# A pre-norm transformer block on one core: the last two MLP sub-units as one group of four tiles, and the attention's GpSimd additions placed one VectorE instruction later

## The chip, the core and the metric

The kernel runs on one core of one Trainium2 chip. A core has five engines that each execute their own queue in order: TensorE (PE in the profile, its weight loads are PEld), VectorE (DVE), ScalarE (ACT), GpSimd (POOL) and SyncE (SP, which here only issues DMAs). They meet through semaphores. The metric is the device time of one execution in microseconds (us).

## The reference

One token stream of 2048 rows and 512 columns goes through a sliding dilated attention and then through an MLP with a squared ReLU, each behind a layer norm and each with a residual.

```python
B, S, D, H, F = 1, 2048, 512, 32, 1792      # head size 16, window 8, dilation 2
qkv = layernorm(x) @ wqkv                    # 2048 x 1536
idx = pos[:, None] - 2 * arange(8)           # eight keys for each row
logits = einsum("bhsd,bhswd->bhsw", q, k[idx]) * 16 ** -0.5   # masked where idx < 0
o = einsum("bhsw,bhswd->bhsd", softmax(logits), v[idx])
h = x + o @ wo
y = relu(layernorm(h) @ w1 + b1) ** 2        # 2048 x 1792
out = h + y @ w2 + b2
```

Everything is float32.

## The kernel before

**Tiles.** The 2048 rows are 16 tiles of 128 rows. Two tiles form a sub-unit `s`, 0 to 7 (`NS` = 8, `RI` = 2 tiles `j` in each). The hidden size of 1792 is 14 blocks `f` (`FB` = 14), the model size 512 is 4 blocks of 128 (`KB`).

**Products in three parts.** Each float32 operand is split into a high part (a cast on ScalarE, `hi`) and a low part (the difference, `lo`), and each product is three: high times high, high times low, low times high. So `mm3` (lines 172 to 177) issues 12 matmuls for 4 blocks. The names in the profile carry this: `hh`, `hl` are the parts of the transposed, normalized h, `rh`, `rl` those of the hidden activations, `oh`, `ol` those of the attention's output, `w_h`, `w_l` those of a weight.

**Phases.** First comes QKV: its products are stored to DRAM (`qkv_d`), and the attention loads windows of them back. The rest is a loop over sub-units (lines 675 to 711). In each, a slot `f` issues on TensorE `mlp1(s, f)` (12 matmuls, the weights stationary, 256 columns moving: both tiles side by side, into a `mm` bank) and, `LAG` = 3 slots behind, `mlp2(s, f - 3)` (6 matmuls of 512 columns into two accumulators `acc0`, `acc1`). Between `mlp1` and `mlp2` of a block stand on ScalarE ReLU, square and the cast `rh` (lines 512, 513, 115), and the difference `rl` on GpSimd (line 118; on VectorE for the last sub-unit, `HV`).

**What a sub-unit does for the next.** In slots 0 and 1 the loads of h, in slots 3 and 4 `o_T`, the transposes of the attention's output of `s + 1` (four PE transposes into a `tr` bank, of which there are two, shared with `wo`), in slots 6 and 7 `wo_product` (12 matmuls of 512 columns), a slot later `h_add` on VectorE with the norm's statistics, the norm's factor `rs` on GpSimd, and three slots after the product `hn` on ScalarE (`h_norm`). In the three slots after the last block `h_T` transposes `hn`, and ScalarE and VectorE make `hh` and `hl`, which the first product of the next sub-unit reads. `finish` (line 544) adds an accumulator to h and stores it; the accumulators exist once, so the next sub-unit's `mlp2` waits for it. `add_b2` adds the bias to h on GpSimd.

**The attention's stream.** `attention()` (lines 219 to 339) is a generator of VectorE work that runs beside the products: for each of 32 items two products with the keys (line 272), two sums (306, 320), softmax pieces, and two products with the values (`weigh`, line 283). What `weigh` makes is added up over the window by three GpSimd instructions, called **additions** here (line 292: two into `pr`, the last into `o`). There are three `pr` buffers. `pump` (line 343) draws from this stream at the end of a slot for as long as the VectorE time that it has counted is below the PE time counted; each piece of the stream counts `SLOW` = 1.1 times its nominal time. `o_T(s)` first draws the stream until sub-unit `s` is complete.

**Order.** The program is written by hand: `at(n, ...)` and `after(n, ...)` put a step into the slot `n` later, ahead of or behind the piece of attention that `pump` draws there. Each engine executes in the order in which its instructions were written.

**Buffers.** Fifteen `row` buffers (`ROWS`) hold h, hn, the parts of o and h, and one piece of w2. The attention has its own: `k`, `v` (2 each), `pr`, `o` (3 each), and the PSUM banks `qp`, `ex`.

Of the kernel before, what the change touches and what calls it, by code (L numbers as in the profile page):

```python
# [15 lines left out]
P = 128  # L16
# [13 lines left out]
LAG = 3  # L30
SLOW = 1.1
DELAY = 3
HV = 7
WJ = 2
# [4 lines left out]
def block_kernel(ctx, tc, x, wqkv, wo, w1, b1, w2, b2, out):  # L39
# [48 lines left out]
    late = {}  # L88
    now = {"slot": 0, "pe": 0.0, "dve": 0.0}

# [128 lines left out]
    def attention():  # L219
# [26 lines left out]
        for n in range(N + 1):  # L246
# [32 lines left out]
            def weigh(j):  # L279
                load_v(n - 1, j)  # L280
                vwin = window(vs[n - 1, j], s1, [DH, GH], [1, DH])
                p2 = att.tile([P, RI, W, GH, DH], F32, name="pr", bufs=3)
                nc.vector.tensor_tensor(  # L283
                    out=p2, in1=vwin, op=ALU.mult,
                    in0=e1[:, :, :, j * GH:(j + 1) * GH].unsqueeze(4).to_broadcast(
                        [P, RI, W, GH, DH]))
                c0 = (2 * gp1 + j) * GC
                w = W // 2
                while w:
                    dst = p2[:, :, :w] if w > 1 else o_t[s1][:, :, c0:c0 + GC].rearrange(  # L290
                        "p i (w h d) -> p i w h d", w=1, h=GH)
                    nc.gpsimd.tensor_tensor(out=dst, in0=p2[:, :, :w], in1=p2[:, :, w:2 * w],  # L292
                                            op=ALU.add)
                    w //= 2
                load_v(n, j)
                done[s1] += 1

# [34 lines left out]
            if new:  # L332
# [21 lines left out]

# [143 lines left out]
    def h_T(s, j):  # L498
        if j == 0:
            hT[s] = ([row("hh", (P, KB // 2, RI, P), F32R) for _ in range(2)],  # L500
                     [row("hl", (P, KB // 2, RI, P), F32R) for _ in range(2)])
        hh, hl = hT[s]
        tr = transposes(hn.pop((s, j)))
        hs_, ls_ = [t[:, :, j] for t in hh], [t[:, :, j] for t in hl]
        due.setdefault(now["slot"], []).insert(0, (hi_T, (tr, hs_)))
        at(0, lo_T, tr, hs_, ls_)

    hid = {}

    def hidden(s, f, ps):  # L510
        r = work.tile([P, RI * P], F32, name="r", bufs=2)
        nc.scalar.activation(r, ps, AF.Relu, bias=b1_sb[:, f:f + 1])  # L512
# [161 lines left out]

    for s in range(NS):
        acc = [psum.tile([P, D], F32, name=f"acc{j}") for j in range(RI)]
        for f in range(FB):
            more = 0.0
            if s + 1 < NS:
                if f in (0, 1):  # L680
                    at(0, load_h, s + 1, f)
                if f in (3, 4):
                    o_T(s + 1, f - 3)
                if f in (6, 7):
                    wo_product(s + 1, f - 6)
                    more = 2.6
            mlp1(s, f)
# [8 lines left out]
        if s + 1 < NS:
            for n, f in enumerate(range(FB - LAG, FB)):
                if n < RI:
                    h_T(s + 1, n)
                    after(0, add_b2, s + 1, n)  # L700
                mlp2(s, f, acc)
                end_slot(1.3)
        else:
            for j in range(RI):
                for f in range(FB - LAG, FB):
                    mlp2(s, f, acc, [j])
                    if j == 0:
                        end_slot(0.65)
        for j in range(RI):
# [25 lines left out]
```

## Time and profile before

| | us |
|---|---|
| median of 3 runs | 533.65 (533.29 to 534.02) |
| the profiled execution | 532.95 |
| its span, first to last instruction | 531.0 |
| sub-unit 1 begins on PE (chain of waits) | 207.67 |
| sub-units 2, 3, 4, 5, 6 | 254.34, 301.02, 347.69, 394.37, 441.04 |
| sub-unit 7 | 487.71 |
| last instruction, an addition on VectorE, ends | 527.93 |

The table's times of sub-units are read from the chain of waits, the list of what released what, followed back from the last instruction. Its pieces are counted there from one engine's release to the next; the timeline of PE counts an instruction from its issue, about 0.16 us earlier. A matmul's duration in the timeline contains its pipeline, so the distance between two starts is what it costs in a row of many. After the last instruction the span contains the store of the last tile.

### The profile page before, as it was taken

The page shows a single profiled execution, that of the slowest core. Times are in us where ns is not written, and L with a number is a line of the kernel's source. Part 1 is how long each engine was busy: PE and PEld are TensorE (multiplying, and loading weights), DVE is VectorE, ACT ScalarE, POOL GpSimd, SP SyncE. Part 2 cuts the span into 40 slices and gives each one's busy share as a digit, 9 for nine tenths or more (in the row PEclk, how much of TensorE's full clock was granted, in tenths as well). Part 3 has the DMA queues.
Part 4 walks back from the last instruction along what each step waited for, and adds up shares of the span by engine and source line. Part 5 has one row for each costly group of instructions (what it writes and reads, how often), then busy time and mean ns, then how long its engine had stood idle before and what let it go on. Part 6 is the DMA issues. An engine that isn't in the chain of part 4 may idle for free.

```text
span 531.0 us, 9020 instructions
## 1 busy us (share of the span) xinstructions
PE 522.5 (98%) x3186; PEld 481.7 (91%) x3186; DVE 376.4 (71%) x569; ACT 262.0 (49%) x607; POOL 319.4 (60%) x435
## 2 busy tenths in 40 slices
PE   7999999999999999999999999999999999999997
PEld 7999999999999878888989898898989889898995
DVE  6569999887888898996998699599869502202111
ACT  4624554455247557455635555563545445254541
POOL 3515489687577389776877777687777834233000
PEclk9999999999999999999999999999999999999999
DMA  8578979687588444633644363364334102001001
GB/s 252 148 234 203 295 236 312 199 270 235 179 241 274 131 145 130 188 103 99 200 134 106 119 185 111 100 191 141 105 110 135 44 0 81 1 0 41 1 1 41
DMA packets 70661, 75.96 MB, mean 143 GB/s; under 512 B 6744, under 2 KB 47704, under 8 KB 70616
## 3 DMA queue, kind: packets, MB, share of 16 engines
q1 hardware_dynamic: 70616, 75.39, 46.8%
q8 instruction: 25, 0.41, 0.3%
q14 instruction: 20, 0.16, 0.1%
HBM read 58.50 MB, written 16.91 MB: 142 GB/s over the span
## 4 chain that ended last, share of the span: by engine, by line
PE 63%; POOL 1%; DVE 0%; issue 0%; POOLq 0%; DVEq 0%
PE mm L177 27%; PE acc L537 27%; PE wo L177 6%; PE tr L155 2%; POOL pr L292 0%; POOL rl L118 0%; DVE pr L283 0%; POOL rs L134 0%; DVE h L544 0%; POOL o L292 0%; POOL rs L136 0%; POOL rs L132 0%; POOLq L118 0%; DVEq L544 0%
## 5 line engine op out<-in xcount | busy, mean ns | idle before, releaser
L292 POOL TENSOR_TENSOR pr<-pr 128x512 f32<-128x512 f32 (+1 forms) x128 | 133.4, 1042 | 49.2 <-DVE pr L283 44.0
L118 POOL TENSOR_TENSOR rl<-r,rh 128x256 fp32r<-128x256 f32 x98 | 73.5, 752 | 80.0 <-ACT rh L115 66.4
L512 ACT ACTIVATE r<-mm,b_sb 128x256 f32<-128x256 f32 x112 | 53.3, 476 | 121.0 <-PE mm L177 117.3
L272 DVE TENSOR_TENSOR pr<-qp,k 128x1024 f32<-128x1024 f32 x64 | 76.0, 1188 | 6.1 <-ACT qp L216 3.5
L283 DVE TENSOR_TENSOR pr<-ex,v 128x1024 f32<-128x1024 f32 x64 | 77.9, 1218 | 2.8
L177 PE MATMUL mm<-hh,w_h 128*128 128x256 f32 x448 | 72.6, 284 | 0.0
L177 PEld LDWEIGHTS mm<-hh,w_h 128*128 128x128 f32 x448 | 66.3, 189 | 6.8 <-ACT r L512 0.4
L177 PE MATMUL mm<-hl,w_h 128*128 128x256 f32 x448 | 72.0, 283 | 0.0
L177 PE MATMUL mm<-hh,w_l 128*128 128x256 f32 x448 | 72.0, 283 | 0.0
L412 ACT COPY y<-mm 128x384 f32<-128x384 f32 x64 | 30.2, 481 | 64.7 <-PE mm L177 35.7
L177 PEld LDWEIGHTS mm<-hl,w_h 128*128 128x128 f32 x448 | 61.8, 192 | 0.0
L177 PEld LDWEIGHTS mm<-hh,w_l 128*128 128x128 f32 x448 | 61.7, 192 | 0.0
L537 PE MATMUL acc<-w_h,rh 128*128 128x512 f32 x192 | 61.3, 400 | 0.0
L537 PE MATMUL acc<-w_h,rl 128*128 128x512 f32 x192 | 60.0, 393 | 1.0 <-POOL rl L118 1.0
L537 PE MATMUL acc<-w_l,rh 128*128 128x512 f32 x192 | 60.0, 392 | 0.0
L177 PE MATMUL mm<-wq_h,xh 128*128 128x384 f32 x256 | 57.1, 344 | 0.0
L177 PE MATMUL mm<-wq_h,xl 128*128 128x384 f32 x256 | 55.6, 338 | 0.4 <-DVE xl L118 0.4
L177 PE MATMUL mm<-wq_l,xh 128*128 128x384 f32 x256 | 55.3, 337 | 0.0
L118 DVE TENSOR_TENSOR hl<-tr,hh 128x256 fp32r<-128x256 f32 x32 | 12.1, 420 | 57.2 <-ACT hh L115 57.2
L513 ACT ACTIVATE r<-r 128x256 f32<-128x256 f32 x112 | 46.8, 418 | 3.5
L115 ACT CAST rh<-r 128x256 fp32r<-128x256 f32 x112 | 45.6, 407 | 3.6
L177 PEld LDWEIGHTS mm<-wq_h,xl 128*128 128x128 f32 x256 | 45.9, 190 | 1.1 <-DVE xl L118 1.1
(76 smaller groups left out, 847.2 us busy)
## 6 DMA issues: line engine op xcount, KB each, us to landing
k<-qkv_d SPq DMA_DIRECT2D x48, 288.0 KB, 2.7
v<-qkv_d SPq DMA_DIRECT2D x48, 288.0 KB, 2.7
qkv_d<-y SPq DMA_DIRECT2D x32, 384.0 KB, 3.5
xt<-in_A_x_dram SPq DMA_DIRECT2D x16, 256.0 KB, 4.3
q<-qkv_d SPq DMA_DIRECT2D x32, 128.0 KB, 2.9
h<-in_A_x_dram SPq DMA_DIRECT2D x16, 256.0 KB, 5.0
out_dram<-h SPq DMA_DIRECT2D x16, 256.0 KB, 3.3
raw<-in_B_w_dram SPq DMA_DIRECT2D x16, 224.0 KB, 4.8
```

Of the source, the lines that this page charges most:

```text
L115: nc.scalar.copy(dst, src)
L118: eng.tensor_tensor(out=dst, in0=src, in1=h, op=ALU.subtract)
L155: nc.tensor.transpose(tr[:, k, :], src[:, k * P:(k + 1) * P], ident)
L177: nc.tensor.matmul(ps, l(k), r(k), start=(n == 0), stop=(n == 3 * KB - 1))
L272: nc.vector.tensor_tensor(out=pr.rearrange("p i w h d -> p i w (h d)"), in0=qp[:, j].unsqueeze(2).to_broadcast([P, RI, W, GC]), in1=kwin, ...
L283: nc.vector.tensor_tensor(out=p2, in1=vwin, op=ALU.mult, in0=e1[:, :, :, j * GH:(j + 1) * GH].unsqueeze(4).to_broadcast([P, RI, W, GH, DH]))
L292: nc.gpsimd.tensor_tensor(out=dst, in0=p2[:, :, :w], in1=p2[:, :, w:2 * w], op=ALU.add)
L412: nc.scalar.copy(y[:, :, t % RI * GC:(t % RI + 1) * GC], ps[:, :3 * GP].rearrange("p (j c) -> p j c", j=6))
L512: nc.scalar.activation(r, ps, AF.Relu, bias=b1_sb[:, f:f + 1])
L513: nc.scalar.activation(r, r, AF.Square)
L537: nc.tensor.matmul(acc[j], l[:, j * P:(j + 1) * P], w[f], start=(f == 0 and n < len(js)), stop=(f == FB - 1 and n >= len(terms) - len(js)))
```

## The change

Sub-units 0 to 5 run as before, with other numbers for the order. Sub-units 6 and 7 (`LAST` = 2) go through `mlp1` and `mlp2` once, as one **wide group** of four tiles: `mlp1` has 512 moving columns instead of 256, `mlp2` issues 12 matmuls into four accumulators, two slots behind (`LAGW`). ReLU, square, cast and difference work on 512 columns; the difference is on VectorE. The parts of h for four tiles lie in the attention's buffers `pr` and `o`, h and hn of sub-unit 7 in `k` and `v`, the two further accumulators in `qp` and `ex`. So `o_T`, `wo_product` and `h_T` of sub-unit 7 move into sub-unit 5 (slots 9 and 10, 11 and 12, and the last two slots behind the blocks), behind those of sub-unit 6, and the attention has to be complete by slot 9 of sub-unit 5.

The additions on GpSimd are written only after the next piece of the stream has been drawn, so behind whatever else `at` or `after` put on GpSimd between. `SLOW` is 1.05 instead of 1.1 from sub-unit 1 on.

```diff
-SLOW = 1.1
+SLOW = 1.1, 1.05
+LAST = 2
+LAGW = 2
-HV = 7
...
-                while w:
...
+                sums.append((p2, o_t[s1], (2 * gp1 + j) * GC, s1))
                 load_v(n, j)
-                done[s1] += 1
...
+    def add_up(p2, o, c0, s):
+        w = W // 2
+        while w:
+            dst = p2[:, :, :w] if w > 1 else o[:, :, c0:c0 + GC].rearrange(
+                "p i (w h d) -> p i w h d", w=1, h=GH)
+            nc.gpsimd.tensor_tensor(out=dst, in0=p2[:, :, :w], in1=p2[:, :, w:2 * w], op=ALU.add)
+            w //= 2
+        done[s] += 1
...
+            todo = sums[:]
+            sums.clear()
             t = next(stream, "end")
+            for a in todo:
+                add_up(*a)
...
-            dve(t * SLOW)
+            dve(t * SLOW[now['sub'] > 0])
...
+        hs[s, j] = row("h") if s < NS - 1 else att.tile([P, D], F32, name="h", tag="k")
...
+        hn[s, j] = row("hn") if s < NS - 1 else att.tile([P, D], F32, name="hn", tag="v")
...
+        if s == NS - LAST and j == 0:
+            parts_ = [att.tile([P, KB // 2, LAST * RI, P], F32R, name=n, tag=tag, bufs=3)
+                      for n, tag in (("hh", "pr"), ("hh", "pr"), ("hl", "pr"), ("hl", "o"))]
+            hT[s] = parts_[:2], parts_[2:]
...
-        at(0, lo, nc.gpsimd if s < HV else nc.vector, rl, r, rh)
+        at(0, lo, nc.vector if wide(s) else nc.gpsimd, rl, r, rh)
...
-        ps = psum.tile([P, RI * P], F32, name="mm", bufs=2)
+        ps = psum.tile([P, (LAST if wide(s) else 1) * RI * P], F32, name="mm", bufs=2)
...
+    def ready_next(s, f):
+        todo = [(s + 1, 0, 3, 6)] + ([(s + 2, 9, 9, 11)] if s == NS - LAST - 1 else [])
+        for n, l, o, w in todo:
+            if f in (l, l + 1):
+                at(0, load_h, n, f - l)
+            if f in (o, o + 1):
+                o_T(n, f - o)
+            if f in (w, w + 1):
+                wo_product(n, f - w)
+                return 2.6
+        return 0.0
...
+            if s == NS - LAST - 1 and f >= FB - RI:
+                h_T(s + 1, f - FB + RI)
+                after(0, add_b2, s + 1, f - FB + RI)
...
+            if s == NS - LAST - 1:
+                if n > 0:
+                    h_T(s + 2, n - 1)
...
+    tags = ["acc0", "acc1", "qp", "ex"]
+    acc = [psum.tile([P, D], F32, name="acc", tag=tag) for tag in tags]
+    js = range(LAST * RI)
+    for f in range(FB):
+        mlp1(s, f)
+        if f >= LAGW:
+            mlp2(s, f - LAGW, acc, js)
+        end_slot(5.4 if f >= LAGW else 2.7)
+    for j in js:
+        for f in range(FB - LAGW, FB):
+            mlp2(s, f, acc, [j])
+            if j == 0:
+                end_slot(0.65)
+        at(0, finish, s + j // RI, j % RI, acc[j])
+        if j:
+            run(due)
```

The change moves instructions at places that the diff alone does not show. The first is GpSimd in sub-unit 0, the differences `rl` of blocks 7 to 12; before, its queue reads:

```order
L118 TENSOR_TENSOR rl<-r,rh 128x256
L132 TENSOR_SCALAR rs<-mv 128x1
L134 TENSOR_TENSOR rs<-rs,mhalf 128x1
L136 TENSOR_SCALAR rs<-mv,rs 128x1
L118 TENSOR_TENSOR rl<-r,rh 128x256
L292 TENSOR_TENSOR pr<-pr 128x2x256
L292 TENSOR_TENSOR pr<-pr 128x2x128
L292 TENSOR_TENSOR o<-pr 128x2x64
L118 TENSOR_TENSOR rl<-r,rh 128x256 x3
```

The same place after the change (line 119 is 118 of before, 343 is 292):

```order
L119 TENSOR_TENSOR rl<-r,rh 128x256
L133 TENSOR_SCALAR rs<-mv 128x1
L135 TENSOR_TENSOR rs<-rs,mhalf 128x1
L137 TENSOR_SCALAR rs<-mv,rs 128x1
L119 TENSOR_TENSOR rl<-r,rh 128x256 x2
L343 TENSOR_TENSOR pr<-pr 128x2x256
L343 TENSOR_TENSOR pr<-pr 128x2x128
L343 TENSOR_TENSOR o<-pr 128x2x64
L119 TENSOR_TENSOR rl<-r,rh 128x256 x3
```

The first row is block 7 in both, the next `rl` block 8; block 9 stood behind the three additions and now stands ahead of them.

The second place is VectorE where sub-unit 4 gives over to 5, around the two pairs `hl` for sub-unit 5. Before:

```order
L320 TENSOR_REDUCE lg<-pr 128x16x4
L118 TENSOR_TENSOR hl<-tr,hh 128x2x128 x2
L283 TENSOR_TENSOR pr<-ex,v 128x1024
L118 TENSOR_TENSOR hl<-tr,hh 128x2x128 x2
L333 TENSOR_REDUCE mx<-lg 128x16
```

After (284, 299, 273 and so on are attention; 119 is the difference):

```order
L284 TENSOR_TENSOR pr<-ex,v 128x1024
L326 TENSOR_REDUCE mx<-lg 128x16
L328 TENSOR_TENSOR lg<-lg,mx 128x128
L273 TENSOR_TENSOR pr<-qp,k 128x1024
L295 TENSOR_REDUCE sm<-ex 128x16
L299 TENSOR_REDUCE lg<-pr 128x16x4
L302 RECIPROCAL sm<-sm 128x16
L273 TENSOR_TENSOR pr<-qp,k 128x1024
L119 TENSOR_TENSOR hl<-tr,hh 128x2x128 x2
L308 TENSOR_TENSOR ex<-ex,sm 128x128
L284 TENSOR_TENSOR pr<-ex,v 128x1024
L119 TENSOR_TENSOR hl<-tr,hh 128x2x128 x2
```

The product with the values that stood between the two pairs `hl` now stands ahead of the first, with seven more pieces of the next item; the two pairs are the same in both.

The third place is ScalarE at the end of sub-unit 5, after the change: the parts `hh` of tile (6, 1), the activations of blocks 12 and 13, then hn and `hh` of tiles (7, 0) and (7, 1), and the first ReLU of the wide group (line 116 casts, 537 and 538 are ReLU and square, 151 is hn):

```order
L116 CAST hh<-tr 128x2x128 x2
L537 ACTIVATE r<-mm,b_sb 128x256
L538 ACTIVATE r<-r 128x256
L116 CAST rh<-r 128x256
L537 ACTIVATE r<-mm,b_sb 128x256
L538 ACTIVATE r<-r 128x256
L116 CAST rh<-r 128x256
L151 ACTIVATE hn<-h,rs 128x512
L116 CAST hh<-tr 128x2x128 x2
L151 ACTIVATE hn<-h,rs 128x512
L116 CAST hh<-tr 128x2x128 x2
L537 ACTIVATE r<-mm,b_sb 128x512
```

Before, the last rows ahead of the next sub-unit's first ReLU there were a pair `hh`, block 13 and a pair `hh`, and the two hn stood four and three blocks ahead of the first `hh`; now each hn of sub-unit 7 stands directly ahead of the `hh` that is made from it, and the second behind the first tile's `hh`.

More of the change, by code (lines that the diff above doesn't have):

```diff
@@ L88, in block_kernel @@
     late = {}
-    now = {"slot": 0, "pe": 0.0, "dve": 0.0}
+    now = {"slot": 0, "pe": 0.0, "dve": 0.0, "sub": 0}
     def at(delta, fn, *a):
@@ L498, in h_T @@
     def h_T(s, j):
-        if j == 0:
+        if s == NS - LAST and j == 0:
+            parts_ = [att.tile([P, KB // 2, LAST * RI, P], F32R, name=n, tag=tag, bufs=3)
+                      for n, tag in (("hh", "pr"), ("hh", "pr"), ("hl", "pr"), ("hl", "o"))]
+            hT[s] = parts_[:2], parts_[2:]
+        elif s < NS - LAST and j == 0:
             hT[s] = ([row("hh", (P, KB // 2, RI, P), F32R) for _ in range(2)],
                      [row("hl", (P, KB // 2, RI, P), F32R) for _ in range(2)])
-        hh, hl = hT[s]
+        u = min(s, NS - LAST)
+        hh, hl = hT[u]
         tr = transposes(hn.pop((s, j)))
-        hs_, ls_ = [t[:, :, j] for t in hh], [t[:, :, j] for t in hl]
+        i = (s - u) * RI + j
+        hs_, ls_ = [t[:, :, i] for t in hh], [t[:, :, i] for t in hl]
         due.setdefault(now["slot"], []).insert(0, (hi_T, (tr, hs_)))
@@ L508, in block_kernel, with wide @@
     hid = {}
+    def wide(s):
+        return s == NS - LAST
     def hidden(s, f, ps):
-        r = work.tile([P, RI * P], F32, name="r", bufs=2)
+        if wide(s):
+            r, rh, rl = row("r"), row("rh", dt=F32R), row("rl", dt=F32R)
+        else:
+            r = work.tile([P, RI * P], F32, name="r", bufs=2)
+            rh = work.tile([P, RI * P], F32R, name="rh", bufs=LAG + 1)
+            rl = work.tile([P, RI * P], F32R, name="rl", bufs=LAG + 1)
         nc.scalar.activation(r, ps, AF.Relu, bias=b1_sb[:, f:f + 1])
         nc.scalar.activation(r, r, AF.Square)
-        rh = work.tile([P, RI * P], F32R, name="rh", bufs=LAG + 1)
-        rl = work.tile([P, RI * P], F32R, name="rl", bufs=LAG + 1)
         hi(rh, r)
-        at(0, lo, nc.gpsimd if s < HV else nc.vector, rl, r, rh)
+        at(0, lo, nc.vector if wide(s) else nc.gpsimd, rl, r, rh)
         hid[s, f] = rh, rl
     def mlp1(s, f):
-        ps = psum.tile([P, RI * P], F32, name="mm", bufs=2)
+        ps = psum.tile([P, (LAST if wide(s) else 1) * RI * P], F32, name="mm", bufs=2)
         fs = slice(f * P, (f + 1) * P)
@@ L526, in mlp1, with mlp2 @@
         at(1, hidden, s, f, ps)
-    def mlp2(s, f, acc, js=range(RI)):
+    def mlp2(s, f, acc, js):
         rh, rl = hid[s, f]
@@ L673, in split_w2 @@
         dve(0.62)
-    for s in range(NS):
+    def ready_next(s, f):
[9 more added lines that the diff above has]
+        return 0.0
+    for s in range(NS - LAST):
         acc = [psum.tile([P, D], F32, name=f"acc{j}") for j in range(RI)]
+        js = range(RI)
+        now["sub"] = s
         for f in range(FB):
[L678 to L686, printed above, removed]
+            more = ready_next(s, f)
+            if s == NS - LAST - 1 and f >= FB - RI:
+                h_T(s + 1, f - FB + RI)
+                after(0, add_b2, s + 1, f - FB + RI)
             mlp1(s, f)
@@ L692, in block_kernel @@
             if f >= LAG:
-                mlp2(s, f - LAG, acc)
+                mlp2(s, f - LAG, acc, js)
                 more += 1.3
             end_slot(1.3 + more)
[L696 to L709, printed above, removed]
-            at(0, finish, s, j, acc[j])
+        for n, f in enumerate(range(FB - LAG, FB)):
+            if s == NS - LAST - 1:
+                if n > 0:
+                    h_T(s + 2, n - 1)
+            elif n < RI:
+                h_T(s + 1, n)
+                after(0, add_b2, s + 1, n)
+            mlp2(s, f, acc, js)
+            end_slot(1.3)
+        for j in js:
+            at(0, finish, s, j, acc[j])
+    s = NS - LAST
+    for j in range(RI):
+        after(0, add_b2, s + 1, j)
+    tags = ["acc0", "acc1", "qp", "ex"]
[6 more added lines that the diff above has]
+        end_slot(5.4 if f >= LAGW else 2.7)
+    for j in js:
+        for f in range(FB - LAGW, FB):
[5 more added lines that the diff above has]
+            run(due)
     run(due)
```

10 lines of the change are left out of this document (1 added, 9 removed).

## The prediction

> **What bounds the kernel now.** First the profile's page: busy shares, the granted clock in the slices, and the shares of the chain of waits.
>
> ```profile
> PE 522.5 (98%) x3186; PEld 481.7 (91%) x3186; DVE 376.4 (71%) x569; ACT 262.0 (49%) x607; POOL 319.4 (60%) x435
> PEclk9999999999999999999999999999999999999999
> PE 63%; POOL 1%; DVE 0%; issue 0%; POOLq 0%; DVEq 0%
> ```
>
> PE is busy for 98% of the span at the full clock, and the chain, followed back for some 65% of the span, is PE with 1% of GpSimd. So the time is the number of matmuls times their distance, plus the few places where PE waits. Then the chain in order of time (start, us, what), for the distances:
>
> ```profile
> 394.37 4.31 PE mm L177 x36
> ...
> 421.91 1.43 PE mm L177 x12
> 423.34 1.39 PE acc L537 x6
> ...
> 448.62 0.44 PE tr L155 x4
> ...
> 454.69 2.72 PE wo L177 x12
> ...
> 484.95 2.76 PE acc L537 x12
> 487.71 5.75 PE mm L177 x48
> ...
> 521.66 5.48 PE acc L537 x24
> 527.24 0.69 DVE h L544
> ```
>
> The reader is to see that nothing but PE stands between 394 and 527 us, and that the rows give prices: 12 narrow matmuls (256 columns) cost 1.43 us or 119 ns each, 12 of `wo` 2.72 us or 227 ns, six of `acc` 1.39 us, twelve in one run 2.76 us, four transposes 0.44 us. That `mm` moves 256 columns and `wo` 512 stands in the groups by line:
>
> ```profile
> L177 PE MATMUL mm<-hh,w_h 128*128 128x256 f32 x448 | 72.6, 284 | 0.0
> L177 PE MATMUL wo<-wo_h,oh 128*128 128x512 f32 x64 | 17.1, 389 | 0.0
> ```
>
> Two narrow ones cost 238 ns, one wide 227.
>
> PE waits in sub-unit 0. Its timeline:
>
> ```profile
> 191.43 0.62 PE L537 MATMUL acc<-w_l,rh 128*128 128x512 f32 x2
> 192.37 0.73 PE L537 MATMUL acc<-w_h,rl 128*128 128x512 f32 x2 [0.31 <-POOL rl L118]
> ...
> 197.72 0.62 PE L537 MATMUL acc<-w_l,rh 128*128 128x512 f32 x2
> 199.05 0.73 PE L537 MATMUL acc<-w_h,rl 128*128 128x512 f32 x2 [0.71 <-POOL rl L118]
> ...
> 201.56 0.62 PE L537 MATMUL acc<-w_l,rh 128*128 128x512 f32 x2
> 202.03 0.62 PE L537 MATMUL acc<-w_h,rl 128*128 128x512 f32 x2
> ```
>
> Undisturbed, these two starts lie 0.47 apart (last pair). They lie 0.94 and 1.33 apart in the others: losses of 0.47 and 0.86 us, to `rl` of blocks 7 and 9.
>
> **Term 1, the wide group.** Sub-units 6 and 7 have 28 slots with 28 x 1.43 = 40.04 us of `mm`. The group has 14 x 12 matmuls of 512 columns, each with weights of its own into one bank like `wo`: 14 x 2.72 = 38.08. Gain 1.96. The 168 `acc` matmuls stay; runs of twelve cost 2.76 where two runs of six cost 2.78, a dozen times: 0.24. Together **2.2 us**. No row shows a wide `mm`; the bounds are 0.24 (as dear as two narrow ones) and 2.4 us (narrow ones by the run of 48, 5.75 us, so 40.25 less 38.08, and 0.24), and I take the `wo` row, which has the same shape and a new weight for each matmul as well. The Trainium skill, page "TensorE: Matmul & The Clock Gate", section "Back-to-back issue gap", gives columns / 2.4 + 2.5 ns for a warm gap. By that, 109.2 and 215.8 ns, joining two saves only the 2.5 ns, an estimate of 0.42 us in all where the rows make 1.96. The trace does not agree for the narrow ones (119 ns), so I stay with the rows.
>
> **Term 2, additions one instruction later.** GpSimd's timeline around the second loss:
>
> ```profile
> 191.58 0.73 POOL L118 TENSOR_TENSOR rl<-r,rh 128x256 fp32r<-128x256 f32 x1
> ...
> 193.92 0.74 POOL L118 TENSOR_TENSOR rl<-r,rh 128x256 fp32r<-128x256 f32 x1
> 194.62 2.62 POOL L292 TENSOR_TENSOR pr<-pr 128x512 f32<-128x512 f32 x2
> 197.31 0.47 POOL L292 TENSOR_TENSOR o<-pr 128x128 f32<-128x128 f32 x1
> 197.73 1.96 POOL L118 TENSOR_TENSOR rl<-r,rh 128x256 fp32r<-128x256 f32 x2
> ```
>
> Block 9's `rl` starts at 197.73 behind 3.1 us of additions. In the new order it stands ahead of them and can start at 194.6, ends near 195.4 and is needed at 198.2. The 0.86 us go. Block 10 comes next behind the additions: they end near 198.5, it near 199.3, needed at 201.2. Block 7 keeps its place behind additions and `rs`, so 0.47 us stay. I take **0.86**; bounds 0 (another `rl` is late instead) and 1.33 (both go).
>
> **Moved at no price: sub-unit 7's o_T, wo and h_T.** They take 4 x 0.44 + 2 x 2.72 = 7.2 us in either place. What has to be ready earlier is the attention. VectorE and GpSimd before:
>
> ```profile
> 390.49 0.76 DVE L118 TENSOR_TENSOR hl<-tr,hh 128x256 fp32r<-128x256 f32 x2 [4.03 <-ACT hh L115]
> 391.17 1.22 DVE L283 TENSOR_TENSOR pr<-ex,v 128x1024 f32<-128x1024 f32 x1
> 392.61 0.76 DVE L118 TENSOR_TENSOR hl<-tr,hh 128x256 fp32r<-128x256 f32 x2 [0.23 <-ACT hh L115]
> ...
> 395.05 1.28 DVE L544 TENSOR_TENSOR h<-acc,h 128x512 f32<-128x512 f32 x2
> ...
> 397.72 1.17 DVE L272 TENSOR_TENSOR pr<-qp,k 128x1024 f32<-128x1024 f32 x1
> ...
> 418.68 1.19 DVE L283 TENSOR_TENSOR pr<-ex,v 128x1024 f32<-128x1024 f32 x1
> ...
> 424.12 0.46 POOL L292 TENSOR_TENSOR o<-pr 128x128 f32<-128x128 f32 x1
> ...
> 395.15 0.64 PE L177 MATMUL mm<-hl,w_h 128*128 128x256 f32 x4
> ```
>
> In the old order the last addition ends at 424.58. Slot 9 of sub-unit 5, where o_T(7, 0) now stands, begins at 421.91, so without more the change would make PE wait 2.7 us there. But the factor 1.05 draws the stream earlier: in the new order eight pieces (391.17 to 397.72, without the `hl` and `h<-acc` between them some 5.5 us) stand ahead of the first `hl`, and both `h<-wo` of sub-unit 6 (some 1.5 us each with their statistics) behind the last piece. From 390.49 the stretch of 29.4 us to 419.87 shrinks by 5.5 + 3.1 to 20.8: the stream ends near 411.3, its additions, 2.6 us with a queue before them, near 414 to 416. Slack some 6 us; price 0.
>
> The other side of drawing early: `hl`, finish and `ol` wait behind more attention, and PE behind them. By the order the pieces ahead of `hl` at the hand-overs to sub-units 2 to 5 are 1.1, 3.2, 4.5 and 5.5 us more than before, so at most some 2.3 us more between one hand-over and the next, and VectorE idles 4.03 us at each (above). It still arrives first. Beyond that PE reads `hl` at 395.15, 1.8 us after 393.37. Price 0. Additions one instruction later also free `pr` later; 0.4 to 1 us a time of the same idle time cover it.
>
> **Term 3, the crowded end of sub-unit 5.** From the prices above, slots counted on from 421.91: wo(7, 1) ends at 436.69, h_T(6, 0) at 437.13, slot 12 at 439.95, h_T(6, 1) at 440.39, slot 13's `mm` at 441.82, two runs of `acc` at 444.60, where h_T(7, 0) wants hn. ScalarE and VectorE pieces:
>
> ```profile
> 436.49 0.65 ACT L115 CAST hh<-tr 128x256 fp32r<-128x256 f32 x2 [3.22 <-PE tr L155]
> ...
> 425.93 0.82 ACT L150 ACTIVATE hn<-h,rs 128x512 f32<-128x512 f32 x1 [1.12 <-POOL rs L136]
> ...
> 521.70 0.48 ACT L512 ACTIVATE r<-mm,b_sb 128x256 f32<-128x256 f32 x1 [1.45 <-PE mm L177]
> ...
> 522.66 0.41 ACT L115 CAST rh<-r 128x256 fp32r<-128x256 f32 x1
> ...
> 523.10 0.43 DVE L118 TENSOR_TENSOR rl<-r,rh 128x256 fp32r<-128x256 f32 x1 [2.39 <-ACT rh L115]
> ```
>
> A block costs ScalarE 1.37 us, a pair `hh` 0.65, hn 0.8. Its queue from 440.43: `hh` to 441.1, blocks 12 and 13 to 443.8, hn(7, 0) to 444.6: on time by nothing. Then h_T(7, 0) to 445.1, its `hh` to 445.8, hn(7, 1) to 446.6, while PE, one run of `acc` later, is at 446.5. I put **0.3 us** of waiting; bounds 0 and 1.5 (`rs` late by as much as the 1.12 shown, and the queue behind it). h_T(6, 1) waits for h_add(7, 1), which VectorE does behind `hl` (6, 0), 438.6, so at 439.3, 0.6 us early. In the group a slot is 5.5 us; ScalarE needs at most 2 x 1.37 and VectorE 2 x 0.43 of it, and the last block's `rl` comes under 3.6 us after its `mm`, when PE has gone through 2.76 + 0.69 + 0.23 = 3.7. Price 0; if it is late, some tenths. The end after the last matmul, 0.69 and the store, is as before.
>
> **Sum.** -2.2 - 0.86 + 0.3 = -2.8 us. The profiled execution took 532.95 (span 531.0), so 530.2 of that kind; the median of the runs shown, 533.65, lies 0.7 higher, which gives **530.8**.
>
> **Rivals.**
> (a) Only the group pays: deferring the additions makes some other `rl` or a `pr` buffer late by what it saves. For it: GpSimd runs strictly in order and additions are often the last thing it waits with. Against: the blocks around 9 have 1.9 us of slack. -2.2 + 0.3 gives 531.8.
> (b) Only the additions pay: a wide `mm` costs what two narrow ones do, 238 ns, since no row shows one with these operands. -0.24 + 0.3 - 0.86 = -0.8, 532.9. By the Trainium skill's page named above ("TensorE: Matmul & The Clock Gate", "Back-to-back issue gap") the sum would be an estimated 532.4, with its 0.42 for 1.96.
> (c) Slower: the attention is not ready for o_T(7, 0). Place: slot 9 of sub-unit 5; PE stands from 421.9 until the last addition has come. If the early draw brought nothing and the end stayed at 424.58 in the old clock, it costs 2.7 and the gain is gone (533.5); each microsecond that VectorE loses on top, through `pr` buffers freed later at 0.4 to 1 us in each of some twenty items, is a microsecond slower. It decides from an end past 424.7; at 427 it is 2.3 us slower, 535.9. Against it speak the 4.03 us of idle time at each hand-over.
> (d) Both losses in sub-unit 0 go and the group's end has no wait: -2.2 - 1.33 = -3.5, 530.1.
>
> **How the numbers follow.** A measurement here can tell some 0.2% (1.07 us) from no change. Chances: forecast 0.57 (530.3 to 531.3), (a) 0.13, (d) 0.10, (b) 0.08, (c) 0.12, of which half about even and half slower. Faster by over 0.2%, below 532.6: forecast, (a), (d) and a little of (b), 0.82. Same: the rest of (b) and half of (c), 0.12. Slower: 0.06. The range leaves out (c) and takes in the others: the lower end is all upper bounds, -2.4 - 1.33 = -3.7, 529.9, with the runs' spread of 0.36 beneath it 529.5; the upper end (b), 532.9.
>
> **What would show it.** After: `mm` with 512 columns at 227 ns from start to start and a slot of 5.48 us (term 1; 119 x 2 refutes it). One wait for `rl` in sub-unit 0 of some 0.3 us, none of 0.7 (term 2). A wait at the second h_T of sub-unit 7 for hn, some tenths (term 3). The last `pr<-ex,v` on VectorE near 411 and the idle time ahead of `hl` halved but not gone. The forecast is wrong if PE shows a wait ahead of o_T or `mm<-hl` in sub-units 1 to 5.

## The result and the profile after

The changed kernel takes 530.66 us, the median of 4 runs (529.56 to 531.34); the kernel before, run beside it, takes 533.80 (533.29 to 534.02). The ratio is 0.9944, 95% interval 0.9933 to 0.9956: 0.56% faster, 3.1 us between the medians and 2.9 between the two profiled executions. A second set of 6 runs (run 10 below) gives 0.9929 (0.9915 to 0.9943). The forecast was 530.8.

The profiled execution of the changed kernel took 530.03 us with a span of 528.3, that of before 532.95 with 531.0. First the busy shares and the granted clock on the page of the changed kernel:

```profile
PE 517.7 (98%) x3018; PEld 469.9 (89%) x3018; DVE 382.7 (72%) x569; ACT 252.1 (48%) x565; POOL 307.3 (58%) x421
PEclk9999999999999999999999999999999999999999
```

PE still bounds the kernel at the full clock. It has 168 instructions fewer and 4.8 us less busy time: 14 blocks with 12 matmuls of 512 columns in place of 28 with 12 of 256. Its chain of waits in order of time (start, us, what):

```profile
207.22 4.31 PE mm L178 x36
...
393.92 4.31 PE mm L178 x36
...
445.01 0.28 POOL rs L137
445.29 0.02 issue
445.31 0.83 ACT hn L151
446.14 0.04 issue
446.18 0.66 PE tr L156 x4
446.84 1.38 PE acc L560 x6
448.22 8.16 PE mm L178 x36
456.38 2.72 PE acc L560 x12
459.11 2.72 PE mm L178 x12
...
516.23 8.17 PE acc L560 x36
...
524.49 0.69 DVE h L567
```

A block of the group costs 2.72 us of `mm` and 2.72 of `acc`, a slot of 5.44. The group lasts from 448.22 to 524.40, 76.18 us; sub-units 6 and 7 without the transposes and `wo` that moved cost 78.90 (from 441.04 to 527.14, less the 7.20 us that moved). Ahead of it PE waits for hn of tile (7, 1); from there the chain leads back over ScalarE and GpSimd to 417 us, while PE itself goes on without a wait. Timeline of PE, then of GpSimd, then of ScalarE, at that place:

```profile
446.18 0.66 PE L156 MATMUL tr<-ident,hn 128*128 128x128 f32 x4 [0.21 <-ACT hn L151]
...
442.65 1.29 POOL L497 TENSOR_TENSOR h<-h,b_sb 128x512 f32<-128x512 f32 x1
...
444.34 0.57 POOL L135 TENSOR_TENSOR rs<-rs,mhalf 128x1 f32<-128x1 f32 x1
445.01 0.27 POOL L137 TENSOR_SCALAR rs<-mv,rs 128x1 f32<-128x1 f32 x1
...
444.61 0.65 ACT L116 CAST hh<-tr 128x256 fp32r<-128x256 f32 x2 [0.75 <-PE tr L156]
445.31 0.82 ACT L151 ACTIVATE hn<-h,rs 128x512 f32<-128x512 f32 x1
```

The hn of (7, 1) needs both: `rs` of its norm, which stands behind the bias addition `h<-h,b_sb` of tile (6, 1) and lands at 445.29, and ScalarE, which is done with `hh` of (7, 0) at 445.26. The transposes that read it come late, by 0.21 us by the profile.

Sub-unit 0, timeline of GpSimd and then of PE:

```profile
192.17 0.73 POOL L119 TENSOR_TENSOR rl<-r,rh 128x256 fp32r<-128x256 f32 x1
...
194.51 1.93 POOL L119 TENSOR_TENSOR rl<-r,rh 128x256 fp32r<-128x256 f32 x2
196.41 2.12 POOL L343 TENSOR_TENSOR pr<-pr 128x512 f32<-128x512 f32 x2
```

```profile
159.76 0.64 PE L178 MATMUL mm<-hh,w_h 128*128 128x256 f32 x4
...
192.96 0.73 PE L560 MATMUL acc<-w_h,rl 128*128 128x512 f32 x2 [0.31 <-POOL rl L119]
...
198.76 0.62 PE L560 MATMUL acc<-w_h,rl 128*128 128x512 f32 x2
```

The `rl` of blocks 8 and 9 stand together ahead of the additions, the wait for block 9 is gone, that for block 7 is still there. The first row of PE is the start of sub-unit 0: 0.59 us later than before (159.17), and nothing in the prediction said so.

The end of the attention, VectorE and GpSimd:

```profile
408.86 2.36 DVE L284 TENSOR_TENSOR pr<-ex,v 128x1024 f32<-128x1024 f32 x2
...
414.96 0.46 POOL L343 TENSOR_TENSOR o<-pr 128x128 f32<-128x128 f32 x1
```

It ends at 411.2 on VectorE and 415.4 on GpSimd, 6 us before o_T(7, 0) wants it (slot 9 of sub-unit 5 begins at 421.46).

So by stretches: start of sub-unit 0 +0.59, sub-unit 0 itself 47.46 instead of 48.50 (-1.04), from the start of sub-unit 1 to that of sub-unit 5 186.70 in both, the end of sub-unit 5 +0.43, the group -2.72, the tail +0.04: -2.7, from 531.0 to 528.3.

### The profile page after: what moved, and what is told of

Read it like the earlier page. It is cut to its first block, busy times and chain, and to the rows that moved or that the text cites. A ratio compares the mean times of both kernels' runs of the same rounds, so it can differ in the third digit from the quotient of the medians.

```text
span 528.3 us, 8621 instructions
## 1 busy us (share of the span) xinstructions
PE 517.7 (98%) x3018; PEld 469.9 (89%) x3018; DVE 382.7 (72%) x569; ACT 252.1 (48%) x565; POOL 307.3 (58%) x421
## 4 chain that ended last, share of the span: by engine, by line
PE 57%; issue 3%; POOL 3%; ACT 0%; DVE 0%; POOLq 0%; DVEq 0%; ACTq 0%
PE mm L178 25%; PE acc L560 25%; PE wo L178 5%; PE tr L156 2%; POOL rl L119 1%; POOL rs L135 1%; POOL h L497 0%; POOL pr L343 0%; DVE pr L284 0%; POOL rs L137 0%; POOL rs L133 0%; ACT hn L151 0%; DVE h L567 0%; ACT r L537 0%; POOL o L343 0%
## 5 line engine op out<-in xcount | busy, mean ns | idle before, releaser
L537 ACT ACTIVATE r<-mm,b_sb 128x256 f32<-128x256 f32 (+1 forms) x98 | 49.6, 506 | 119.5 <-PE mm L178 110.6
L119 POOL TENSOR_TENSOR rl<-r,rh 128x256 fp32r<-128x256 f32 x84 | 62.5, 748 | 57.3 <-ACT rh L116 57.3
L178 PE MATMUL mm<-hh,w_h 128*128 128x256 f32 (+1 forms) x392 | 69.8, 300 | 0.0
L178 PE MATMUL mm<-hl,w_h 128*128 128x256 f32 (+1 forms) x392 | 69.0, 298 | 0.0
L178 PE MATMUL mm<-hh,w_l 128*128 128x256 f32 (+1 forms) x392 | 68.9, 298 | 0.0
L178 PEld LDWEIGHTS mm<-hh,w_h 128*128 128x128 f32 x392 | 59.9, 189 | 6.8 <-ACT r L537 0.2
L178 PEld LDWEIGHTS mm<-hl,w_h 128*128 128x128 f32 x392 | 56.8, 191 | 2.2
L119 DVE TENSOR_TENSOR rl<-r,rh 128x512 fp32r<-128x512 f32 x14 | 9.7, 692 | 59.8 <-ACT rh L116 59.8
L178 PEld LDWEIGHTS mm<-wq_l,xh 128*128 128x128 f32 x256 | 45.3, 188 | 0.6 <-DVE wq_l L119 0.6
L538 ACT ACTIVATE r<-r 128x256 f32<-128x256 f32 (+1 forms) x98 | 44.0, 449 | 3.1
```

The lines of the kernel that those rows point to most:

```text
L119: eng.tensor_tensor(out=dst, in0=src, in1=h, op=ALU.subtract)
L178: nc.tensor.matmul(ps, l(k), r(k), start=(n == 0), stop=(n == 3 * KB - 1))
```

## The experiments

Eleven runs follow. Runs 1, 2 and 4 to 7 are the changed kernel with one part altered, 8, 9 and 11 with several, 10 is the changed kernel itself, and 3 starts from the kernel before. The table gives for each the median, the ratio to the kernel before on the same chip with its interval, and the stretches of its profiled execution, in us: the start of sub-unit 0 (first `mm<-hh`), sub-unit 0, from the start of sub-unit 5 to that of the group, and the group up to its last matmul. From the start of sub-unit 1 to that of sub-unit 5 all thirteen profiles show 186.66 to 186.70. The first limit is read from the timeline of PE and the others from the chain of waits, so every length of sub-unit 0 holds the same 0.16 us too much.

| kernel | median | ratio (interval) | start of 0 | sub-unit 0 | 5 to group | group |
|---|---|---|---|---|---|---|
| before | 533.80 | 1 | 159.17 | 48.50 | | |
| changed | 530.66 | 0.9944 (0.9933, 0.9956) | 159.76 | 47.46 | 54.30 | 76.18 |
| 1 additions at once | 531.10 | 0.9964 (0.9951, 0.9977) | 159.36 | 48.50 | 54.52 | 76.17 |
| 2 factor 1.1 | 536.46 | 1.0060 (1.0047, 1.0073) | 159.63 | 47.45 | 60.08 | 76.18 |
| 3 without the group | 532.49 | 0.9988 (0.9979, 0.9996) | 159.61 | 47.46 | | |
| 4 `mm` in halves | 532.22 | 0.9980 (0.9972, 0.9989) | 159.87 | 47.45 | 54.30 | 78.66 |
| 5 end of sub-unit 5 | 529.53 | 0.9928 (0.9915, 0.9942) | 160.73 | 47.46 | 53.87 | 76.17 |
| 6 `rs` later | 529.58 | 0.9929 (0.9913, 0.9945) | 159.54 | 47.25 | 54.32 | 76.17 |
| 7 biases later | 529.52 | 0.9922 (0.9909, 0.9936) | 159.25 | 47.46 | 54.30 | 76.18 |
| 8 = 5 + 6 + 7 | 529.32 | 0.9919 (0.9903, 0.9934) | 160.15 | 47.26 | 53.88 | 76.17 |
| 9 = 8, hn and xt moved | 528.82 | 0.9909 (0.9896, 0.9922) | 158.39 | 47.03 | 53.87 | 76.17 |
| 10 changed, again | 530.16 | 0.9929 (0.9915, 0.9943) | 159.93 | 47.47 | 54.30 | 76.17 |
| 11 group alone | 534.22 | 1.0010 (1.0001, 1.0020) | 159.83 | 48.50 | 58.28 | 76.19 |

The stretches behind the start of sub-unit 0 repeat within 0.04 us where nothing was altered in them; the start itself moves by over 2 us. Effects of some tenths are therefore read from the stretches, and the medians, with intervals of 0.2 to 0.3%, only bear out their sum. The medians come from several sets on more than one chip, in which the kernel before took 533.26 to 533.80 us; between rows the ratios compare better.

### 1. The additions at once

```diff
-                sums.append((p2, o_t[s1], (2 * gp1 + j) * GC, s1))
+                add_up(p2, o_t[s1], (2 * gp1 + j) * GC, s1)
```

> The changed kernel with one part undone: the three additions on GpSimd are written at once behind the product with the values, as before the change. Theory (the deferral pays in sub-unit 0, because block 9's rl no longer stands behind 3.1 us of additions): a wait of PE for rl of 0.7 us (0.86 us lost) is back near 199, the one of 0.31 near 193 stays, sub-unit 1 begins 0.9 to 1.0 us later counted from the start of sub-unit 0, sub-units 1 to 5 keep their length of 186.70 us together, and the time rises by 0.9 to 1.0 us to 531.6 (ratio 0.996 to the kernel before). Rival (the deferral is of no use, rather it cost the 0.59 us that the changed kernel lost ahead of sub-unit 0): sub-unit 0 begins near 159.2 instead of 159.76, and the time is 530.1 to 530.7. Rival two (what the deferral gained is only in the order that the faster stream made): no wait for rl comes back and the time stays at 530.7.

Timeline of PE of this run:

```profile
199.24 0.74 PE L560 MATMUL acc<-w_h,rl 128*128 128x512 f32 x2 [0.72 <-POOL rl L119]
```

The wait is back, and sub-unit 0 lasts 48.50 us as before the change: the deferral is worth 1.04 us there. Another 0.2 us come back early in sub-unit 5. The ratio is 0.9964, as expected (0.996); the median lies 0.5 us below the 531.6 expected, and so does the median of the kernel before in this set, 533.26 for 533.80. The start of sub-unit 0 is 0.40 earlier, toward the rival's 159.2, but not the time; what the deferral has to do with the start is taken up in the account of the prediction below.

### 2. The old factor

```diff
-SLOW = 1.1, 1.05
+SLOW = 1.1, 1.1
```

> The changed kernel with the factor 1.1 on the attention's pieces in every sub-unit, so that the attention is no longer drawn early. Theory (the early draw is what makes the attention ready for o_T(7, 0) in slot 9 of sub-unit 5): the last addition on GpSimd lands near 424 as before the change, PE waits for it at the transposes of o_T(7, 0) by 2 to 2.7 us, behind 421.9, and the time rises to 532.7 to 533.4 (ratio 0.998 to 1.0 to the kernel before); VectorE again idles some 4 us ahead of hl at the hand-overs. Rival (the order alone, in which the second tile's h<-wo comes behind the stream, makes it early enough): no wait of PE there, time 530.7 as changed. A third way (the late draw also pushes hn of sub-unit 7): over 533.4.

Timeline of GpSimd, then of PE:

```profile
416.61 0.22 POOL L133 TENSOR_SCALAR rs<-mv 128x1 f32<-128x1 f32 x1
...
418.63 0.74 POOL L119 TENSOR_TENSOR rl<-r,rh 128x256 fp32r<-128x256 f32 x1 [0.78 <-ACT rh L116]
...
422.06 0.22 POOL L133 TENSOR_SCALAR rs<-mv 128x1 f32<-128x1 f32 x1
...
423.26 2.06 POOL L343 TENSOR_TENSOR pr<-pr 128x512 f32<-128x512 f32 x2
425.40 0.46 POOL L343 TENSOR_TENSOR o<-pr 128x128 f32<-128x128 f32 x1
```

```profile
425.91 0.47 PE L156 MATMUL tr<-ident,o 128*128 128x128 f32 x1 [4.29 <-POOL o L343]
426.04 1.20 PE L178 MATMUL mm<-hh,w_h 128*128 128x256 f32 x4
427.04 1.05 PE L178 MATMUL mm<-hh,w_l 128*128 128x256 f32 x4
```

Neither of the first two outcomes: PE waits where the theory put it, but 4.29 us, and the time is 536.46, above the kernel before. That is the time of the third way, but not its mechanism: PE waits 0.23 us for hn, where the changed kernel waits 0.21. The first term is the queue of GpSimd: the `rs` of both `h<-wo`, 1.2 us each, and an `rl` for which GpSimd waits 0.78 us now stand ahead of the deferred additions, where before the change one `rs` and an `rl` without a wait did. So the last one ends at 425.86, 32.1 us after the start of sub-unit 5, where before the change it was 30.2. The second is the clock. Busy time by stretch, PE alone (us from and to, length, busy and number of matmuls, granted clock, DMA share, GB/s):

```profile
421.70:425.80 4.10, 0.00 (x0) 0.95 0.00 0
425.90:427.10 1.20, 1.19 (x6) 0.50 0.00 0
...
428.70:430.10 1.40, 1.40 (x8) 0.98 0.00 0
```

After the wait the granted clock is 0.50 for 2.8 us, and the 12 `mm` take 2.7 us in place of 1.43. 4.29 and 1.28 make 5.57 of the 5.78 us by which the stretch of sub-unit 5 grew; the span grew by 5.6.

### 3. Everything but the group

In the kernel before:

```diff
-SLOW = 1.1
+SLOW = 1.1, 1.05
...
+            todo = sums[:]
+            sums.clear()
             t = next(stream, "end")
+            for a in todo:
+                add_up(*a)
...
-            dve(t * SLOW)
+            dve(t * SLOW[now['sub'] > 0])
...
```

> The kernel before with the deferral of the additions and the factor 1.05, but without the group: sub-units 6 and 7 go through the MLP one after the other, o_T, wo and h_T of sub-unit 7 stay in sub-unit 6. Theory (the parts add up): the gain is that of the wait for rl of block 9 alone, 0.9 to 1.0 us less than before, so 532.7 (ratio 0.998); a slot of sub-units 6 and 7 costs 1.43 and 1.39 us and both last 39.5 us, no wait at the end of sub-unit 5, and the difference to the changed kernel is 2.72 - 0.43 = 2.3 us. Rival (the group's price and the draw hang together, without the group the earlier stream delays h_add or ol): 533.0 or more with a wait of PE in sub-units 1 to 5.

Sub-unit 0 again lasts 47.46 us. From the start of sub-unit 5 to the last matmul it is 132.78 us (393.76 to 526.54), before the change 132.77, after it 130.48: the group with its crowded end is worth 2.30 us, as expected, and in these stretches the factor 1.05 costs and brings nothing of itself. The start of sub-unit 0 is 0.44 later than before.

### 4. The wide product in halves

```diff
-        mm3(ps, lambda k: w1_h[:, k, fs], lambda k: w1_l[:, k, fs],
-            lambda k: hh[k // 2][:, k % 2], lambda k: hl[k // 2][:, k % 2])
+        n = LAST if wide(s) else 1
+        for c in range(n):
+            part = slice(c * RI, (c + 1) * RI)
+            mm3(ps[:, c * RI * P:(c + 1) * RI * P],
+                lambda k: w1_h[:, k, fs], lambda k: w1_l[:, k, fs],
+                lambda k: hh[k // 2][:, k % 2, part], lambda k: hl[k // 2][:, k % 2, part])
```

> The changed kernel with the first product of the group in two halves: each block's 12 matmuls of 512 columns become 24 of 256 columns, first those of the tiles of sub-unit 6 into one half of the bank, then those of sub-unit 7 into the other. Everything else of the group is as changed, also two runs of 6 acc as one run of 12. Theory (the gain of the group is the price of a wide mm, 2.72 instead of 2 x 1.43, and the rest the alternation of short runs): a block's mm costs 2.82 to 2.86 us instead of 2.72, the group is 14 x 0.10 to 0.14 = 1.4 to 2.0 us longer, time 532.1 to 532.7 (ratio 0.997 to 0.998); a run of 12 acc again costs 2.76 if it is the passage between runs of 256 and of 512 columns that costs 0.03 to 0.04, and 2.72 if it is not. Rival (the width is worth nothing, the whole 2.72 come from fewer passages and from waits): time 530.7 to 531.0.

Its chain of waits:

```profile
448.29 8.64 PE mm L178 x72
456.93 2.75 PE acc L564 x12
459.68 2.87 PE mm L178 x24
462.55 2.75 PE acc L564 x12
```

The same work in narrow matmuls costs 2.87 us a block, and the same 12 `acc`, untouched by the edit, 2.75 instead of 2.72. The group grows by 2.48 us: `mm` 0.48 for the first three blocks and 11 x 0.15, together 2.1; `acc` 11 x 0.03 and 0.03 at the end, together 0.4. So the width carries 2.48 of the 2.72 us, and a change between runs of 256 and of 512 columns costs some 0.03 us in the `acc` run behind it. That the width is worth nothing (rival (b) of the prediction) falls. The halves double the matmuls and their weight loads together, so which of the two the price hangs on stays open.

### 5 to 8. What is left

The changed kernel itself did not run in the set of these four, so its median can't be set against theirs; the stretches of the profiles can.

Run 5, the end of sub-unit 5:

```diff
-                after(0, add_b2, s + 1, f - FB + RI)
+                after(2, add_b2, s + 1, f - FB + RI)
-        after(3, h_norm, s, j)
+        after(2 if (s, j) == (NS - 1, 1) else 3, h_norm, s, j)
```

Run 6, `rs` and hn of sub-unit 1:

```diff
-            after(0, finish)
+            after(1 if isinstance(key, tuple) and key[0] == 1 else 0, finish)
-        after(3, h_norm, s, j)
+        after(4 if s == 1 else 3, h_norm, s, j)
```

Run 7, the loads of the biases, in `first_phase` instead of the loop ahead of it:

```diff
-        if n == 13:
-            consts()
...
+            if (t0, n) == (6, 1):
+                consts()
```

> The changed kernel with another order at the end of sub-unit 5: the bias additions add_b2 for the tiles of sub-unit 6 come two slots later on GpSimd, behind the factors rs of sub-unit 7's norm, and hn of tile (7, 1) one slot earlier, so directly behind hn of (7, 0) on ScalarE and ahead of the pairs hh of sub-unit 7. Theory (the 0.43 us at the end of sub-unit 5 come from the bias additions and rl ahead of rs on GpSimd, and from hn(7, 1) behind hh(7, 0)): no wait of PE for hn, 54.3 us from the start of sub-unit 5 to that of the group become 53.87, and the time falls by 0.4 us (ratio 0.9936). Rival (the wait only moves, to hh or hl ahead of the group's first product, since ScalarE has the same work): 54.2 to 54.3 us there, time 530.7 as changed.

53.87 us in place of 54.30, and no wait for hn: the 0.43 us are named and gone. The run moved `rs` and hn together; in the changed kernel `rs` lands at 445.29 and ScalarE is done with `hh` of (7, 0) at 445.26, so which of the two alone would have been enough stays open.

> The changed kernel with, for sub-unit 1's norm alone, the three GpSimd instructions of rs written one slot later, so behind the rl of block 7 and of block 8, and hn written for both tiles in the slot in which the second was (the first one slot later). Theory (what is left of the waiting in sub-unit 0 is the rl of block 7 behind rs, 0.47 us, and 0.1 us of restart): no wait of PE for rl, sub-unit 0 lasts 46.9 us instead of 47.46, time down by 0.5 (ratio 0.9935). Rival (the additions, not rs, are what rl of block 7 waits for, or the next rl is late instead): 47.3 to 47.5 us and the time as changed.

Sub-unit 0 lasts 47.25 us: 0.21 of the expected 0.5. The wait for `rl` is gone, and a new one stands two blocks on, in the timeline of PE:

```profile
195.87 0.74 PE L178 MATMUL mm<-hh,w_h 128*128 128x256 f32 x4 [0.16 <-ACT r L537]
```

ScalarE has the softmax's `ex` (waiting for VectorE until 194.44) and hn ahead of that ReLU, and in the changed kernel, where PE comes 0.5 us later, the same ReLU ends at 196.12, 0.28 ahead of the product at 196.40. The rival had it half right: the next one was late, but on another engine.

> The changed kernel with the loads of the two biases b1 and b2 (b2 is written to all 128 partitions, 256 KB) issued later, in the QKV products of tiles 6 and 7 instead of between the last products of the first four tiles, so that SyncE issues the load of x for tile 7 and the stores of y some 2 us earlier. Theory (the 0.3 to 0.6 us that some runs lose at the x transposes near 60 us, 59.84 to 60.5 in the runs so far, come from DMAs that land late behind these loads, not from the change): the stretch from the transposes near 44 us to those near 60 us is at the lower end of what the runs showed, 15.7 to 15.8 us, with no wait there, and sub-unit 0 begins 0.3 to 0.5 us earlier than in the changed kernel; time 530.2 to 530.7. Rival (the loads of biases are beside the point, and what varies is the start of the run): the stretch stays between 15.7 and 16.4 us, and so does the time at 530.7.

The stretch from the x transposes near 44 us to those near 60 us is 15.81 us, sub-unit 0 begins at 159.25, 0.51 earlier than in the changed kernel, and 529.52 us is less than either outcome had. But profiles with the loads where they were show 15.74 (before) and 15.86 (run 10), so the length of the stretch doesn't show a gain. What it shows is the wait: in the changed kernel VectorE waits 1.09 us for the load of x tile 7, before the change 0.47, in run 10 0.82; here it doesn't, nor in runs 8 and 9. But run 8 has the same loads and takes 16.41 for the stretch: there a copy `y` on ScalarE, 5.68 us behind the second x transposes, waited for its store, where in run 7 the same copy came at 5.17 and waited for PE alone. So the wait for the load of x is settled, the stores are not.

> The changed kernel with the orders of the last three runs together: bias additions and hn at the end of sub-unit 5, rs and hn of sub-unit 1, and the later loads of the biases. Theory (the three losses are apart from each other and PE has no other wait behind sub-unit 0's start): 0.43 + 0.5 us less than the changed kernel, and 0.2 to 0.5 us of the start, so 529.3 to 529.8 (ratio 0.992 to 0.993), and no wait of PE over 0.2 us from 64 us on. Rival (one removed wait makes the next engine late): 530.0 to 530.7 with a wait that names it.

47.26 and 53.88 us, both as the single runs had them: the losses are apart. The time, 529.32, lies in the range expected, with run 6's new wait still in it and a late start of sub-unit 0.

### 9 and 10. The combined order and the changed kernel once more

On top of run 8, hn of sub-unit 1 and the norm of x tiles 6 and 7:

```diff
-        after({(1, 0): 4, (1, 1): 4, (NS - 1, 1): 2}.get((s, j), 3), h_norm, s, j)
+        after({(1, 0): 5, (1, 1): 5, (NS - 1, 1): 2}.get((s, j), 3), h_norm, s, j)
...
-                if n in (4, 5):
-                    at(0, x_norm, t0 - 2 + n)
+                if n in ((2, 3) if t0 == R else (4, 5)):
+                    at(0, x_norm, t0 - 2 + n + 2 * (t0 == R))
```

> The kernel with the three orders together (end of sub-unit 5, rs of sub-unit 1, loads of the biases), and on top hn of sub-unit 1 two slots later than in the changed kernel (behind one more block's ReLU, square and cast on ScalarE) and, in the QKV products of tiles 4 and 5, the norm of the x tiles 6 and 7 two slots earlier on ScalarE, so ahead of the copies y that wait for a store. Theory (what the last run of three orders still lost in sub-unit 0, 0.3 us, is the ReLU behind hn and ex on ScalarE; and the x transposes near 60 us are late because xt stands on ScalarE behind a copy y that waits 4.6 us for a DMA): sub-unit 0 lasts 46.8 to 46.9 us with no wait of PE, the stretch from the second transposes near 46.9 us to those near 60 us is 13.2 us, time 528.3 to 528.9 (ratio 0.990 to 0.991). Rival (the copies themselves, which the x tile no longer holds up, or a later rl make PE wait): 529.0 to 529.5.

> The changed kernel itself once more, beside the combined orders on the same chip. Theory (the 0.59 us that it lost ahead of sub-unit 0 in its first profile are variation from run to run, in the start and in DMAs that land early or late): the stretch from the second transposes near 46.8 us to those near 60 us and the start of sub-unit 0 come out elsewhere within 13.2 to 14.6 us and 159.2 to 160.7 us, all stretches behind that repeat within 0.05 us (47.46, 186.70, 54.30 and 76.18 us), ratio 0.9935 to 0.995. Rival (it is the change): sub-unit 0 begins at 159.7 to 159.8 again.

Run 9: sub-unit 0 lasts 47.03 us and has no wait that the profile names (expected 46.8 to 46.9), the second x transposes near 46 and those near 60 lie 13.09 apart (expected 13.2; before the change 13.21, run 10 13.33), no other wait of PE follows. It is the fastest of all, 528.82 us, 0.9909 (0.9896 to 0.9922) against 0.9929 (0.9915 to 0.9943) of the changed kernel on the same chip. The stretches account for 0.43 + 0.44 us; the intervals overlap a little, so the rest of the 1.34 us between the medians isn't shown.

Run 10: all stretches behind the start repeat within 0.01 us, the stretch from the second x transposes to those near 60 us is 13.33 (expected 13.2 to 14.6), and the start is 159.93, neither 159.17 nor 159.76. The ratio, 0.9929, lies just below the 0.9935 to 0.995 expected.

### 11. The group alone

Both edits of runs 1 and 2 together.

> The changed kernel with the factor 1.1 everywhere and the additions written at once: of the change only the group is left, with nothing that draws the attention earlier. Theory (in the run with the factor 1.1 alone, the last additions came 1.9 us later than before the change, since the rs of sub-unit 6's norm then stood ahead of them on GpSimd, and the clock fell after so long a wait): now the last addition ends 30.2 us after the start of sub-unit 5, as before the change, PE waits 2.4 us for it at o_T(7, 0) instead of 4.29, and if the granted clock falls to a half again, another 1.3 us go; sub-unit 0 is 1.04 us longer. Time 530.7 + 1.04 + 2.4 = 534.1 without a fall of the clock, 535.4 with one. Rival (the deferral has no part in the wait): 4.3 us of waiting again, and 536.4 to 537.5.

The last addition ends at 425.14, 30.15 us after the start of sub-unit 5 (30.2 before the change), and PE waits 2.31 us for it: the other 2 us of run 2 were the deferral. Timeline of PE:

```profile
425.19 0.47 PE L156 MATMUL tr<-ident,o 128*128 128x128 f32 x1 [2.31 <-POOL o L343]
425.31 1.20 PE L178 MATMUL mm<-hh,w_h 128*128 128x256 f32 x4
426.31 1.05 PE L178 MATMUL mm<-hh,w_l 128*128 128x256 f32 x4
```

Granted clock of PE behind the wait, columns as in run 2:

```profile
424.90:426.00 1.10, 0.81 (x4) 0.54 0.00 0
426.00:427.60 1.60, 1.60 (x10) 0.50 0.00 0
```

The clock falls here too. With it the stretch of sub-unit 5 is 3.98 us longer than in the changed kernel: the wait, 1.28 and 0.15 for the `mm` and the `acc` behind it, and the 0.2 of run 1. The median, 534.22 us, lies between the two times expected, 534.1 without a fall of the clock and 535.4 with one. The profiled execution, in which it fell, is the longest of the ten, 535.12, so whether it falls after such a wait each time isn't shown. With a ratio of 1.0010 (1.0001 to 1.0020) the group by itself is no gain at all. Run 1, which differs from this one by the factor alone, stands at 0.9964: the factor 1.05 is what makes the group a gain.

## Why the prediction was right

The forecast of 530.8 met 530.66, and its reasons hold; but the sizes of all three terms were too small, on balance by 0.57 us of gain, and in the profile a shift at the start that no term held was about as large. That the total met the forecast so closely is in part luck.

**Term 1, the wide group: right, and too small.** Predicted -2.2, measured -2.72, outside the bound of 2.4 that the prediction gave the term. The 227 ns of the `wo` row were right to the digit for the wide `mm` (2.72 us for 12). By the two chains the `mm` of sub-units 6 and 7 fell from 40.1 to 38.1 us, 2.0 where 1.96 stood. Nearly all of the miss is `acc`: "runs of twelve cost 2.76" was read from a place behind a narrow run; between wide ones they cost 2.72. All `acc` of the two sub-units fell from 38.8 to 38.1 us, and the 0.24 became 0.7.

**Term 2, the deferral: right, and too small.** Predicted -0.86, measured -1.04 (runs 1 and 3, both ways). The place, the block and what stays were as predicted. The 0.86 were taken from the distance between two starts; the products behind a wait are slower for a moment as well (0.73 for 0.62 us, and 1.47 for 1.43 in the chain of before), which a distance that ends at the start of the waiting matmul doesn't hold. These make 0.15 of the missing 0.18.

**Term 3, the crowded end: right in place and sign.** Predicted +0.3, measured +0.43. The prediction had hn(7, 1) late behind `hh` on ScalarE; the trace puts `rs` on GpSimd, behind `rl` and the bias addition of (6, 1), last by 0.03 us. Run 5, which moved both, took the wait away.

**What was priced at nothing was nothing.** The attention ended at 411.2 and 415.4 (predicted 411.3, 414 to 416); sub-units 1 to 4 kept their length to the hundredth; VectorE's idle time ahead of the first `hl` fell from 4.03 to between 2.27 and 3.57 us, so less than by half.

**Rival (c) was real, and underpriced.** Without the early draw it cost 5.6 us of the span and ended on the other side, 1.0060. Its mechanism and place were right (run 2). Its price of 2.7 us missed two things: the deferral itself moves the last additions behind one more `rs` and a wait for `rh` (2 us), and PE came back from the wait at half the clock (1.3 us). That the early draw brings enough was read from the order of the pieces, which was the right place to look.

**Not in the prediction: the start.** The 0.59 us ahead of sub-unit 0 are in no term. In the ten profiles whose products of QKV are unaltered (all but runs 7, 8 and 9) the start of sub-unit 0 lies at 159.17, 159.36 and 159.83 with the additions at once, and at 159.54 to 160.73 with them deferred. The two overlap, but these starts alone can't exclude that some tenths belong to the deferral. Against it speaks the place: 0.13 us of the 0.59 are there by the second x transposes near 46.7 us and all of it by the ones near 60, and up to there GpSimd runs its additions and `rs` in the same order before and after the change. Between these two transposes a load of x and the stores of `y` land early or late. What makes these DMAs land differently from run to run is open. For the forecast it means that 0.57 us of gain too small and 0.59 us of this start happened to cancel in the profiled execution. In the set of run 10 the medians differ by 3.45 us, nearer to the 3.33 that the stretches behind the start make than to the 2.8 of the forecast.

## What to carry to other kernels

Where PE bounds a kernel, read the price of a matmul as the distance of starts in a run of the same shape and between the same neighbours; a block of 512 columns here costs 0.15 us less than two of 256, and its neighbours gain as well. A group that needs its input earlier is only worth its price together with the order that delivers it: here the group alone was no faster than the kernel before, and with the old factor the whole change was 0.6% slower. Once a wait is removed, look for the instruction that it hid, on every engine that feeds the same matmul.

## What the runs showed of the hardware

**A wait of PE costs more than itself.** After 4.29 us of waiting the granted clock was 0.50 for 2.8 us (run 2), after 2.31 us at 0.50 to 0.54 for about as long (run 11), some 1.3 us on top in each (12 `mm` in 2.71 us for 1.43). The Trainium skill, page "TensorE: Matmul & The Clock Gate", section "Part 1: The HAM clock gate (the "warmup" mystery)", has the clock at half after an idle window of about 3.4 us and at full after a busy one. The half clock agrees; the 2.8 us at half are shorter than the page's window, and that a wait must last 3.4 us doesn't agree, since 2.31 us were enough in the profiled execution. The wait of 0.71 us in sub-unit 0 of the kernel before left no such mark: the granted clock is 1.00 from 195 to 202 us. At the start of the program waits shorter than 2.31 us were enough: in run 1 PE waits 1.41 and then 1.11 us, with four transposes between, and the granted clock is 0.50 from 8 to 10 us; the changed kernel, with waits of 1.23 and 0.45 us there, shows 1.00.

**Neighbours of another width cost 0.03 us.** Twelve `acc` of 512 columns take 2.72 us between wide `mm` and 2.75 between narrow ones, with the same operands and no wait (run 4).
